# A chunked attention and feed-forward kernel: the second block's first pair is transposed by VectorE, and four small edits at the start

## The chip, the cores and the metric

One Trainium2 chip, one of its cores. The time is that of one execution on the device, in microseconds; the kernel before was timed in three runs. One further execution was profiled, and all rows below come from it. Shorter is better.

## The reference

```python
# q, k, v: 8 batches x 8 heads x 576 tokens x 64, float32
scores = (1 / sqrt(64)) * q_c @ k_c.T          # in chunks of 64 tokens
scores = scores - max(scores, axis=-1)
attn   = exp(scores)
attn   = attn / (sum(attn, axis=-1) + 1e-9)
x      = (attn @ v_c).transpose(...).reshape(4608, 512)
h      = x @ w_in                              # w_in: 512 x 2048, float64
g      = h * (1 / (1 + exp(-1.702 * h)))
out    = g @ w_out                             # w_out: 2048 x 512, float64
```

Attention runs inside chunks of 64 tokens. Its result is the input of a two-layer feed-forward net. The weights come in 8-byte words, and the kernel turns them into a high and a low 4-byte part itself.

## The kernel before, in words

The 4608 tokens are 36 tiles of 128, in 9 blocks of 4 tiles. Every large product is done in three passes (high weight with low data, high with high, low with high). The first three blocks are computed plainly: for each of 16 column tiles j of the hidden layer, `h_j` makes 128 hidden features for 512 tokens (two halves, `h0_j` and `h_j`, six products each, lines L1607 to L1609), ScalarE and VectorE turn them into `g` (steps `gh` and `gl`, L1628, L1629, L1633), and four steps `o_j_t` (L1643 to L1645, three products each) add the second layer's part for tile t. The other six blocks go in pairs of blocks with fewer products; the change does not touch them.

The weights are fetched once, one tile j of `w_in` and one of `w_out` at a time, and are prepared during the first block. A weight's steps are: `raw_j` (SP issues its transfers, L373 and L378), `wsc_j` and `wlow_j` on ScalarE (L382, L389), `wshift_j` and `wj_j` on VectorE (L395, L402), `wh_j` on ScalarE (L418), `w_j` on VectorE (L421). Tiles 0 and 1 are handled in two parts, `raw_0_0` (`w_in`) and `raw_0_1` (`w_out`). `w_15` is the last one, and `h0_15` needs it.

Attention of the first block is done in four units (`plan_first`), of two heads and 512 tokens each: `q_u`, `k_u`, `v_u` are transfers (L507, L528), `tqp_u` and `tkp_u` transposes on TensorE by products with an identity (L541 for units 0 and 2, L549 for units 1 and 3), `s_u` the scores (L579), then the largest value, the subtraction, the exponential, the sum (`s_sum`, which adds `eps` = 1e-9, L596), the normalising on GpSimd, `ep_u` a transpose back (L606), `xp_u` the product with v (L628). Before the first transposes TensorE runs 7 warming products, ident by ident, of 128 columns (`keep_warm`, L1720), whose result nobody uses.

From the second block on, attention goes in pairs u of token tiles, all heads at once (`plan_pair`). The constant `NPE` says which pairs use TensorE for their transposes: those with u below 6, which is pair 4 alone. Pair 4 loads rows of q and k in 4 transfers of 256 KB (L478), transposes them on TensorE in two steps of eight (`tp0_4`, `tp1_4`, L1353), copies the results out (`tq`, L1360 on ScalarE, `tk`, L1363 on VectorE), computes scores (`s_4`, L1387), transposes e with eight products (`ep_4`, L1423) that ScalarE copies out (L1427), and multiplies by v in a step of its own (`xp_4`, L1461). All later pairs load q and k in small pieces of 32 KB (`load_qk`, L1328), so placed that VectorE's 32 x 32 transposes do the rest (`t_dve`, L1371, two instructions; `e_dve`, L1436, eight instructions), and their product with v runs directly behind the scores of the next pair (`s_u` takes `last["x"]` with it) into the two `hp` banks of PSUM.

The order of all steps is one list of names, `ORDER`, written out at the top; each step issues its instructions on its own engine's queue, and every queue runs in order. All transfers are issued by SP. A step only waits for what it reads, and for the buffers that it overwrites; buffers are matched by a tag. The first weight part's buffer for j = 1 has the tag `w1a`.

Of the kernel before, what the change touches and what calls it, by code (L numbers as in the profile page):

```python
# [8 lines left out]
F32 = mybir.dt.float32  # L9
# [5 lines left out]
ALU = mybir.AluOpType  # L15
AX = mybir.AxisListType
# [221 lines left out]
def tile_chunk_attention_ffn(  # L238
# [21 lines left out]
    NB = NTL // TB  # L260
    BT = TB * P
    SCALE = 1.0 / float(D) ** 0.5
    NPE = 6
    NTMP = 3
    WARM = 7
    FILL = ()
# [1519 lines left out]
```

## Time and profile before

| | us |
|---|---|
| median of three runs (lowest, highest) | 813.99 (812.33, 816.24) |
| the profiled execution's own time | 814.22 |
| its span, first to last instruction | 812.4 |
| TensorE busy | 803.3 |
| VectorE busy | 595.0 |
| ScalarE busy | 380.3 |
| GpSimd busy | 90.0 |

The engine's busy time is the time in which it has an instruction running; the ends of matmuls are modelled. The share of TensorE is 99%, of VectorE 73%, of ScalarE 47%, but these are means over stages that differ. The granted clock of TensorE is 1.0 in every slice that the page shows.

### The profile page before, as it was taken

The numbers are of one execution on the slowest core, as the hardware profiler recorded it, in microseconds if no ns is written. First come the engines' busy times: TensorE is split into PE (matmuls) and PEld (weight loads), VectorE is DVE, ScalarE is ACT, GpSimd is POOL, SyncE is SP. The second block draws the span as 40 slices with busy tenths as digits, with TensorE's granted clock in tenths as the row PEclk, the third lists the DMA queues.
The fourth block names the chain that finished last, engine by engine and source line by source line (L and its number), as shares of the span: only waits on it lengthen the run. The fifth ranks groups of instructions, "written<-read, shape, count | busy, mean of one in ns | idle before, by whom it ended". The sixth has DMA issues, their size and how long they took to land.

```text
span 812.4 us, 15467 instructions
## 1 busy us (share of the span) xinstructions
PE 803.3 (99%) x5934; PEld 666.6 (82%) x5934; DVE 595.0 (73%) x900; ACT 380.3 (47%) x610; POOL 90.0 (11%) x83
## 2 busy tenths in 40 slices
PE   7999999999999999999999999999999999999998
PEld 6788888888888888888888888888888888888887
DVE  4888974646567979886787888876878545659965
ACT  5998934334445546413345451523554512338450
POOL 1100004030045651000000010000001000000000
PEclk9999999999999999999999999999999999999999
DMA  9995646642366677667664538676533046766433
GB/s 266 301 349 127 160 94 182 166 97 52 66 186 169 172 198 215 179 184 216 180 159 130 133 80 217 178 215 192 156 118 105 0 128 193 230 202 220 134 100 105
DMA packets 240106, 133.17 MB, mean 164 GB/s; under 512 B 179104, under 2 KB 207776, under 8 KB 240032
## 3 DMA queue, kind: packets, MB, share of 16 engines
q1 hardware_dynamic: 240032, 132.18, 58.0%
q8 instruction: 47, 0.77, 0.4%
q14 instruction: 27, 0.22, 0.1%
HBM read 97.52 MB, written 32.51 MB: 160 GB/s over the span
## 4 chain that ended last, share of the span: by engine, by line
PE 97%; DMA 1%; ACT 0%; issue 0%; DVE 0%; SPq 0%; DVEq 0%
PE po L1643 13%; PE po L1645 13%; PE po L1644 13%; PE hp L867 9%; PE hp L869 9%; PE hp L868 9%; PE hp L1607 5%; PE hp L1609 5%; PE hp L1608 5%; PE acc_A L1133 3%; PE acc_B L1133 3%; PE s L1387 2%; PE x L1461 2%; PE acc_A L1126 2%; PE acc_B L1126 1%; DMA first_a<-in_k_dram 1%
## 5 line engine op out<-in xcount | busy, mean ns | idle before, releaser
L1643 PE MATMUL po<-w,g_l 128*128 128x512 f32 x448 | 176.4, 394 | 0.0
L1645 PE MATMUL po<-w,g_h 128*128 128x512 f32 x448 | 174.5, 390 | 0.0
L1644 PE MATMUL po<-w,g_h 128*128 128x512 f32 x448 | 174.5, 389 | 0.0
L1643 PEld LDWEIGHTS po<-w,g_l 128*128 128x128 f32 x448 | 84.1, 188 | 18.4 <-DVE g_l L918 0.4
L1645 PEld LDWEIGHTS po<-w,g_h 128*128 128x128 f32 x448 | 84.1, 188 | 17.6
L1644 PEld LDWEIGHTS po<-w,g_h 128*128 128x128 f32 x448 | 84.1, 188 | 16.9
L867 PE MATMUL hp<-w,w 128*128 128x512 f32 x224 | 87.5, 390 | 0.1
L869 PE MATMUL hp<-w,w 128*128 128x512 f32 x224 | 87.2, 389 | 0.0
L868 PE MATMUL hp<-w,w 128*128 128x512 f32 x224 | 87.2, 389 | 0.0
L1436 DVE STREAM_TRANSPOSE eT<-e 32x512 f32<-32x512 f32 x120 | 84.2, 702 | 3.1 <-POOL e L1417 1.2
L1417 POOL TENSOR_TENSOR e<-e,r 128x1024 f32<-128x1024 f32 x16 | 31.5, 1968 | 436.4 <-DVE r L1414 338.9
L1607 PE MATMUL hp<-x_l,w 128*128 128x512 f32 x184 | 72.1, 392 | 0.0
L1608 PE MATMUL hp<-x_h,w 128*128 128x512 f32 x184 | 71.6, 389 | 0.0
L1609 PE MATMUL hp<-x_h,w 128*128 128x512 f32 x184 | 71.6, 389 | 0.0
L1628 ACT ACTIVATE hp<-hp 128x512 f32<-128x512 f32 x48 | 28.0, 584 | 81.6 <-PE hp L1609 71.5
L1633 DVE TENSOR_TENSOR g_l<-hp,g_h 128x512 fp32r<-128x512 f32 x48 | 33.0, 688 | 44.9 <-ACT g_h L1629 44.6
L867 PEld LDWEIGHTS hp<-w,w 128*128 128x128 f32 x224 | 42.1, 188 | 9.9 <-issue 0.5
L869 PEld LDWEIGHTS hp<-w,w 128*128 128x128 f32 x224 | 42.0, 188 | 8.7
L868 PEld LDWEIGHTS hp<-w,w 128*128 128x128 f32 x224 | 42.0, 188 | 8.6
L867 PE MATMUL hp<-w,pieces 128*128 128x512 f32 x112 | 43.7, 390 | 0.0
L869 PE MATMUL hp<-w,pieces 128*128 128x512 f32 x112 | 43.6, 389 | 0.0
L868 PE MATMUL hp<-w,pieces 128*128 128x512 f32 x112 | 43.6, 389 | 0.0
(225 smaller groups left out, 1473.3 us busy)
## 6 DMA issues: line engine op xcount, KB each, us to landing
w<-seven SPq DMA_DIRECT2D x112, 256.0 KB, 3.1
pieces<-seven SPq DMA_DIRECT2D x56, 256.0 KB, 3.2
seven<-w SPq DMA_DIRECT2D x24, 512.0 KB, 3.7
raw<-in_moe_w_in_dram SPq DMA_DIRECT2D x16, 512.0 KB, 7.2
raw<-in_moe_w_out_dram SPq DMA_DIRECT2D x16, 512.0 KB, 6.9
four<-four_w SPq DMA_DIRECT2D x32, 256.0 KB, 3.5
raw<-in_q_dram SPq DMA_DIRECT2D x208, 32.0 KB, 2.2
raw<-in_k_dram SPq DMA_DIRECT2D x208, 32.0 KB, 2.2
```

Of the source, the lines that this page charges most:

```text
L867: nc.tensor.matmul(hp, w[:, 0, c], xl[:, c], start=c == 0, stop=False)
L868: nc.tensor.matmul(hp, w[:, 0, c], xh[:, c], start=False, stop=False)
L869: nc.tensor.matmul(hp, w[:, 1, c], xh[:, c], start=False, stop=c == 1)
L1133: nc.tensor.matmul(halves(o), gh[:, c], w, start=first, stop=stop, skip_group_check=not fresh)
L1436: nc.vector.transpose(st["et"][po : po + 32, :, 32 * a : 32 * a + 32], st["e"][pi : pi + 32, :, 32 * b : 32 * b + 32],)
L1607: nc.tensor.matmul(hp, wh, xl, start=cc == 0, stop=False)
L1608: nc.tensor.matmul(hp, wh, xh, start=False, stop=False)
L1609: nc.tensor.matmul(hp, wl, xh, start=False, stop=cc == NCC - 1)
L1633: nc.vector.tensor_tensor(gl, h_t[g], gh.bitcast(F32), op=ALU.subtract)
L1643: nc.tensor.matmul(po, gl[:, c], w[:, 0, :], start=first, stop=False)
L1644: nc.tensor.matmul(po, gh[:, c], w[:, 0, :], start=False, stop=False)
L1645: nc.tensor.matmul(po, gh[:, c], w[:, 1, :], start=False, stop=last)
```

## The change

Seven edits in one:

1. `NPE` goes from 6 to 4. Pair 4 takes the way of the later pairs: 32 small transfers for q and k, transposes on VectorE, its product with v behind the scores of pair 6. The list loses `rows0_4`, `rows1_4`, `tp0_4`, `tp1_4`, `tk0_4`, `tk1_4`, `ep_4`, `xp_4` and gains `qk_0_0_4` to `qk_1_3_4`, `et0_4` to `et2_4`, `hp0_6`, `hp1_6`.
2. The warming becomes 14 products of 64 columns.
3. A tile `hold` with the tag `w1a` gets a copy of the lower right quarter of the identity. The last transposing product of k_0 reads it, so the transfer `raw_1_0`, whose buffer has the same tag, cannot start before that product is done. The step also names `tkp_0` as a need.
4. `eps` becomes a part of a larger tile; the sums of the first block are reduced into row 0 of a two-row view whose row 1 holds 1e-9, and a second reduction adds the rows, in place of an addition.
5. The need of a pair's transposes on those of the pair before is dropped for pair 4, which no longer has one before it on that path.
6. Part 0 of weight 0 becomes the first weight that is loaded.
7. `ORDER` is written anew from end to end. Its transfers begin: before `q_0 k_0 k_1 q_1 raw_1_0 q_2 k_2 k_3 q_3 raw_2 v_0 v_1 raw_0_0 v_2 v_3`, after `q_0 k_0 q_1 k_1 raw_0_0 q_2 k_2 k_3 raw_1_0 q_3 raw_2 v_1 v_0 raw_0_1 qk_0_0_4 v_2 v_3`. TensorE's steps begin: before `warm tqp_0 tkp_0 tkp_1 tqp_1 s_0 s_1 tqp_2 tkp_2 tkp_3 tqp_3 s_2 s_3`, after `warm tqp_0 tkp_0 tqp_1 tkp_1 s_0 tqp_2 s_1 tkp_2 tkp_3 tqp_3 s_2 s_3`. The rest of the list differs in many places by a step or two.

```diff
-    NPE = 6
+    NPE = 4
...
-    WARM = 7
+    WARM = 14
...
-    eps = pad.tile([P, 96], F32, tag="pad", name="eps")[:, :16]
+    small = pad.tile([P, 96], F32, tag="pad", name="small")
+    eps = small[:, :16]
+    zeps = small[:, 32:64].rearrange("p (r c) -> p r c", r=2)
...
-    nc.vector.memset(eps, 1e-9)
+    nc.vector.memset(small, 1e-9)
+    hold = const.tile([P, 1024], F32, tag="w1a", name="hold")[:, :CH]
+    nc.vector.tensor_copy(hold[CH:], ident[CH:, CH:])
...
-            plan.add(DMA, (n, 1.5, 384), at - 5.5, load, need=slot_users(j), make=e("raw"), take=[tag])
+            plan.add(DMA, (n, 1.5, 384), at - 5.5, load, need=slot_users(j) + ["tkp_0"] * (name == "1_0"), make=e("raw"), take=[tag])
...
-                            nc.tensor.matmul(to, data, ident[r, r], start=True, stop=True)
+                            last = (u, i, t, h, half) == (0, 1, TB - 1, 1, 1)
+                            nc.tensor.matmul(to, data, hold[r] if last else ident[r, r], start=True, stop=True)
...
-            nc.vector.tensor_reduce(z, st["e"], axis=AX.X, op=ALU.add)
-            nc.vector.tensor_tensor(z, z, eps[:, :NK], op=ALU.add)
+            nc.vector.tensor_reduce(zeps[:, 0, :NK], st["e"], axis=AX.X, op=ALU.add)
+            nc.vector.tensor_reduce(z, zeps[:, :, :NK].rearrange("p r c -> p c r"), axis=AX.X, op=ALU.add)
...
-        warm = pool.tile([P, P], F32, tag=tag, name="warm")
+        warm = pool.tile([P, CH], F32, tag=tag, name="warm")
         for _ in range(count):
-            nc.tensor.matmul(warm, ident, ident, start=True, stop=True)
+            nc.tensor.matmul(warm, ident, ident[:, :CH], start=True, stop=True)
```

## Rows read from the trace of the kernel before

**Rows 1.** The page: busy time and instructions of each engine; an instruction queue.

```profile
PE 803.3 (99%) x5934; PEld 666.6 (82%) x5934; DVE 595.0 (73%) x900; ACT 380.3 (47%) x610; POOL 90.0 (11%) x83
...
q8 instruction: 47, 0.77, 0.4%
```

**Rows 2.** Windows, first 26 us: length, then busy us of PE, PEld, DVE, ACT, POOL.

```profile
0.00:26.00 26.00, 20.25 (x478) 17.24 (x482) 14.43 (x32) 15.69 (x26) 4.87 (x10) 1.00 0.90 265
```

**Rows 3.** Waits of PE over the whole span: total, times, longest.

```profile
PE qkTp L541 <- issue: 2.0, 1, 2.0
```

**Rows 4.** Chain that ended last, 8 to 20 us: start, us, what.

```profile
11.67 1.98 issue
```

**Rows 5.** Timeline of PE and SP, first 20 us: start, us, instructions, idle before.

```profile
1.36 3.36 PE L1720 MATMUL warm<-ident 128*128 128x128 f32 x14 [1.36 <-POOL ident masks.py:199]
...
5.21 0.67 SPq L507 DMA_DIRECT2D first_a<-in_q_dram  x1
6.99 1.97 PE L549 MATMUL qkTp<-ident,first_a 128*64 128x128 f32 x32 [1.00 <-DMA first_a<-in_k_dram]
...
8.06 4.79 SPq L528 DMA_DIRECT2D first_b<-in_v_dram  x4
...
19.62 0.69 PE L628 MATMUL x<-first_b 64*64 64x64 f32 x32 [0.25 <-ACT first_b L613]
```

**Rows 6.** Windows: busy PE, PEld, DVE, ACT, POOL; clock, DMA share, GB/s.

```profile
30.00:116.00 86.00, 85.99 (x684) 70.80 (x683) 73.39 (x87) 70.68 (x88) 4.14 (x3) 1.00 0.70 205
50.00:60.00 10.00, 10.00 (x104) 8.11 (x104) 9.64 (x11) 9.33 (x12) 0.00 (x0) 1.00 1.02 363
80.00:100.00 20.00, 20.00 (x148) 16.40 (x147) 18.63 (x21) 18.80 (x22) 0.00 (x0) 1.00 0.67 180
64.00:68.00 4.00, 4.00 (x19) 3.30 (x19) 3.09 (x6) 3.96 (x6) 1.91 (x1) 1.00 0.33 53
26.00:30.00 4.00, 4.00 (x36) 3.20 (x26) 4.00 (x7) 3.89 (x8) 0.00 (x0) 1.00 1.00 342
```

**Rows 7.** Chain that ended last, at the detours of pairs 4 and 8.

```profile
31.06 0.88 PE qkTp L1353 x8
...
31.95 0.50 PE hp L1607
...
68.30 0.23 PE po L1645
68.53 0.87 PE eTp L1423 x8
...
75.54 1.09 PE x L1461 x64
76.63 0.43 PE hp L1607
...
113.27 0.93 PE x L1461 x64
```

**Rows 8.** Timeline of DVE and PE around the last weight tile.

```profile
114.60 1.23 DVE L421 TENSOR_TENSOR w<-wtmp,w 128x1024 fp32r<-128x1024 f32 x1 [1.12 <-ACT w L418]
...
116.09 0.39 PE L1645 MATMUL po<-w,g_h 128*128 128x512 f32 x1
116.48 0.50 PE L1607 MATMUL hp<-x_l,w 128*128 128x512 f32 x1
```

**Rows 9.** Groups of instructions of VectorE, first 116 us: busy, mean ns, idle before.

```profile
L1436 DVE STREAM_TRANSPOSE eT<-e 32x512 f32<-32x512 f32 x8 | 5.6, 697 | 0.1
L1371 DVE STREAM_TRANSPOSE qkT<-raw 128x1024 f32<-128x1024 f32 x4 | 4.8, 1230 | 0.0
L1363 DVE COPY qkT<-qkTp 128x512 f32<-128x512 f32 x2 | 1.4, 683 | 0.0
```

**Rows 10.** Line L1328: issue of a small transfer, ns min/median/max.

```profile
L1328 SPq DMA_DIRECT2D raw<-in_k_dram x208: 312/449/2570, 62.0 to 559.0; - x104
```

**Rows 11.** The page: transfers, KB each, median us from issue to landing.

```profile
first_b<-in_v_dram SPq DMA_DIRECT2D x8, 128.0 KB, 5.0
```

More of the change, by code (lines that the diff above doesn't have):

```diff
@@ L1517, in plan_pair @@
                 plan.add(
-                    DVE, 1.14, rank, lambda i=i: t_dve(i), need=raw[i * NP : i * NP + NP] + ([ev("tq0")] if i else [f"tq1_{u - 2}"]),
+                    DVE, 1.14, rank, lambda i=i: t_dve(i), need=raw[i * NP : i * NP + NP] + ([ev("tq0")] if i else [f"tq1_{u - 2}"] * (u > TB)),
                     make=ev(f"tq{i}"), take=[] if i else ["tr"], give=[raw_tag] if i else (),
```

350 rows, old and new, of the table ORDER are left out of this document.

## The prediction

> **What bounds the kernel now.** I read the page first: TensorE is busy for 803.3 of 812.4 us [rows 1], so little can be won but less TensorE work, or less idle time at the two ends. The windows put 5.75 of the 9.1 us of idleness into the first 26 us (26.00 minus 20.25) [rows 2]; the other 3.4 lie nearly all behind the last product, in the last addition and store, where the change only shuffles a few steps, and I leave them as they are. At the start the waits and the chain name the largest piece: 2.0 us of "issue" inside the transposes of unit 2 (L541), from 11.67 on [rows 3, 4]. "Issue" is a wait for nothing that the profile shows. By the code TensorE had then run 14 warming records and 64 + 32 + 64 + 48 more, 222, each with its own weight load, so 444 instructions; the page has 47 transfers of 16 KB on an instruction queue, and 2 x 5934 instructions over 47 transfers is one per 252 [rows 1]. I therefore take the 1.98 us for a late code transfer that shared the DMA engines with weights. A further 1.0 us is the wait for the k of unit 1, until 6.99 [rows 5].
>
> From 26 us on TensorE has no gap, but VectorE has little room: in the stretch 30 to 116 us, in which all weights are split and the second block's attention runs, it is busy 73.4 of 86 us while TensorE is busy 85.99 [rows 6]. The last weight tile shows how close this is: VectorE finishes w_15 at 114.60 + 1.23 = 115.83, and h_15 starts at 116.48, 0.39 after the start of a product that normally hands over after 0.23 [rows 7, 8]: it waits 0.16 us. So before 116 us a saving on TensorE is worth only what VectorE can follow.
>
> **The change part by part.** The sum is made against the profiled execution, 814.22 us (span 812.4 and 1.8 around it), 0.23 above the median of 813.99.
>
> Pair 4 leaves TensorE's transposes. A detour is worth its chain pieces plus what the next product takes beyond the usual 0.23 [rows 7]: the first eight transposes 0.88 + (0.50 - 0.23) = 1.15; the second eight have no such follower and are like the eight of e, 0.87 each. The products x_4 stood alone, 1.09 + (0.43 - 0.23) = 1.29; they now ride behind s_6, where the same 64 cost 0.93, so 0.36 less. Together 3.25 us of TensorE work, all of it before h_15.
>
> What it adds on VectorE: eight 32-row transposes of e at 0.697 (5.6) and two of q and k at 1.230 (2.5), less two copies of 0.683 (1.4): 6.7 us more, all of it in the order ahead of w_15 [rows 9]. ScalarE loses three copies. x_4 now leaves through both hp banks; the pairs after it do so in the chain with no wait, so nothing is put down for it [rows 7].
>
> VectorE decides what the 3.25 us are worth. It has 86 - 73.4 = 12.6 us idle in the stretch. For the full gain it must do 73.4 + 6.7 = 80.1 us of work in 86 - 3.25 = 82.75, which is 97% busy. Its densest rows are 9.64 of 10 us (96.4%) and 18.63 of 20 (93.2%) [rows 6]. At 96.4% the work takes 83.1 us, a gain of 2.9; at 93.2% it takes 85.9, a gain of 0.1. I take the middle, 95%: 84.3 us, a gain of 1.7, with 0.1 and 3.25 as ends.
>
> The loads of pair 4's q and k become 32 transfers of 32 KB in place of 4 of 256 KB. SP issues such a one in 0.449 us [rows 10], 14.4 us in all, spread between weight loads; the DMA engines need more too: the stretch with only such transfers moved 53 GB/s at a share of 0.33, so 161 GB/s at full share against 342 [rows 6], that is 6.5 us in place of 3.1 for 1.05 MB. These 3.4 us fall where the DMA share is 1.0 and delay weights; no ScalarE or VectorE step of the weights waits for its transfer now (they wait for one another, as w_15 does), so I price them at nothing and keep up to 3.4 us for the case that this cover goes.
>
> The first 26 us. The warming becomes 14 products of half the width. Seven of 128 columns took 3.36 us [rows 5]; with time by columns 14 of 64 take the same, with time by product twice that. The bounds are 3.4 and 6.7 us, and I take 3.4, since records of the same shape later need only 0.87 / 8 = 0.11 each [rows 7] where these took 0.24, so it is the streaming and not the number of them that was slow. Up to 1.0 us more would vanish in the wait that ends at 6.99. The Trainium skill (TensorE: Matmul & The Clock Gate, section "The mechanism") says a weight load overlaps running products only where the row groups differ; with full-array weights each product then costs load plus stream, and by its figures (section "LDWEIGHTS") the warming would take an estimated 4.5 us, still inside that wait. The 0.24 us of the warming row fits that rule and the hidden load alike, and the sum is 811.5 us by both.
>
> The 28 more instructions ahead of the first transposes move the code boundary of instruction 444 to the start of tkp_2, and TensorE asks for that code a little sooner. The held-back load adds a wait on SP: raw_1_0 starts only when the last transposed product of k_0 is done, near 6.0 us, where SP issued q_3 at 5.21 [rows 5]; q_3, raw_2 and the v of units 1 and 0 stand behind it. For that time no weight is put in front of the code transfer. The stall can go by 0 to 2.0 us. But a half-megabyte weight now also stands ahead of q_3 and v: 1.5 to 2 us. The four v issues ended at 8.06 + 4.79 = 12.85 [rows 5] and such a transfer lands 5.0 us after its issue [rows 11], at 17.9; that becomes about 19.5, and x of unit 0 ran at 19.62 [rows 5]. So what the stall gives is mostly taken back by v. I take 1.0 us, between 0 and 2.0.
>
> The Trainium skill (DMA: Bandwidth & Descriptors, section "Queues, rings and completion order") says each DMA engine takes turns between its queue rows, a packet at a time. By that rule the code transfer does not stand behind SP's backlog and holding a weight back buys nothing; the sum would lose its 1.0 us. The 1.98 us row fits queueing better, but shows no queue.
>
> The 1e-9 as a second row: a small addition becomes a reduction of 16 values, four times; the larger memset and the copy into "hold" run before VectorE has its first input, the transposes of unit 1, which start at 6.99 [rows 5]. Nothing either way.
>
> Sum: 814.2 - 1.7 - 1.0 = 811.5 us.
>
> **The rivals.** *All of it arrives.* VectorE reaches 97% and the code stall goes whole: 814.2 - 3.25 - 2.0 = 808.9. For it: TensorE went through 50 to 60 us without a gap while VectorE was at 96.4% [rows 6]. Against it: no row shows VectorE at 97% for 80 us.
>
> *VectorE takes the gain back.* It stays at 93% and the v transfers or the code transfer eat the start: 814.2 - 0.1 - 0 = 814.1. The row of 80 to 100 us speaks for it.
>
> *Slower: VectorE's idle time doesn't shrink.* Its queue is in order, and its 12.6 us are waits for ScalarE and TensorE results; if they stay, w_15 comes 6.7 us later, h_15 starts at 123.2, the removed TensorE work only becomes waiting, and the time is 814.2 + 6.7 = 820.9. It decides from the point where more than 5.9 us of the 12.6 remain idle (12.6 - 6.7: above this h_15 starts later than now); each further us costs one. For it: h_15 waits for w_15 even now. Against: ScalarE has less to do, and much of the idleness is VectorE waiting for a TensorE that is behind it.
>
> *The warming takes twice as long.* 3.36 us more, of which the wait of 1.0 before 6.99 takes up 1.0: 811.5 + 2.4 = 813.9.
>
> **How the numbers follow.** Forecast 0.42 (809.9 to 813.2); all arrives 0.28 (807.8 to 809.9); taken back 0.15 (813.2 to 815); slower 0.09 (815 to 821); doubled warming 0.06. A measurement here can tell about 0.5% (4.1 us, so 809.9 and 818.1) from no change. Faster by more: the second case and a sliver of the first, 0.33. Slower by more: the far half of the slower case, 0.05. Within: 0.62. The range leaves out the lower edge of "all arrives" and most of "slower": 807.8 to 815.8.
>
> **What would show it.** TensorE's total should fall by about 3.2 us, with 24 transposes of 128 columns gone; if not, the first step is wrong. The "issue" wait in L541 or its neighbours should be under 1.5 us. VectorE from 30 us to the end of w_15 should be about 95% busy; h_15 should start near 113.5 to 114. TensorE waits on w (L421) or g_l before 116 us, over 4 us in sum, would mean the slower case. A wait of x (L628) for v would confirm the price of the hold. Matmul starts 0.24 us apart in the warming mean that it doubled.

## The result, and the profile after

The changed kernel takes 819.76 us (median of six runs, 818.58 to 821.50); the kernel before, on the same chip, 814.73. The ratio is 1.0077, with an interval of 1.0062 to 1.0092: slower, by 5 to 7.5 us. (The ratio is not that of the two medians, which is 1.0062; here and below the two can lie 0.15% apart.) The forecast was 811.5, and the range ended at 815.8. The profiled execution took 820.12 us, with a span of 818.3 against 812.4.

The page after, in the lines that answer to [rows 1], and the windows that answer to [rows 2, 6] (length; busy us of PE, PEld, DVE, ACT, POOL; clock, DMA share, GB/s):

```profile
PE 807.6 (99%) x5924; PEld 669.5 (82%) x5924; DVE 601.3 (73%) x909; ACT 378.8 (46%) x607; POOL 93.2 (11%) x83
```
```profile
0.00:26.00 26.00, 21.86 (x426) 20.18 (x426) 12.75 (x30) 14.53 (x24) 4.69 (x10) 0.99 0.83 240
30.00:116.00 86.00, 85.19 (x643) 68.58 (x646) 78.53 (x96) 68.48 (x84) 4.60 (x2) 1.00 0.75 209
```

TensorE has lost 24 transposes, and yet it is busy 4.3 us longer. VectorE is busy 78.5 us between 30 and 116 us in place of 73.4, and TensorE, which had no gap there, now has 0.8 us of them. The waits of TensorE over the span (total, times, longest):

```profile
PE po L1650 <- DVE g_l L1640: 2.3, 3, 1.7
PE eTp L613 <- POOL first_b L608: 2.0, 2, 1.8
...
PE hp L1614 <- DVE x_l L1482: 0.4, 1, 0.4
```

The gaps over 0.15 us between 30 and 120 us are waits for VectorE: for a g_l at 74 and at 105 us (0.24 and 0.39), and for the x_l of h_15 at 119. The longest ones lie elsewhere, 1.8 us at 23 us (for GpSimd) and 1.7 at 295 us. The issue wait of [rows 3] is gone. The start is told by the timeline of TensorE (start, us, instructions, idle before), to be read against [rows 5]:

```profile
1.36 6.24 PE L1727 MATMUL warm<-ident 128*128 128x64 f32 x28 [1.36 <-POOL ident masks.py:199]
...
9.45 3.22 PE L556 MATMUL qkTp<-ident,first_a 128*64 128x128 f32 x32
...
25.14 0.66 PE L613 MATMUL eTp<-ident,first_b 128*128 128x128 f32 x4 [1.82 <-POOL first_b L608]
...
27.40 1.92 PE L635 MATMUL x<-first_b 64*64 64x64 f32 x64
```

The warming has the 28 records of 0.22 us, nearly as long as those of twice the width before (0.24). The transposes of unit 1 (L556) take 3.22 us where they took 1.97 [rows 5], and the same line later in this kernel takes 1.97 again. Behind the wait of 1.82 us, 64 products of L635 take 1.92 us (1.45 before). The windows there show why: the granted clock is at half, the lower of the two levels (1.2 GHz), from 25.7 to 29.1 us.

```profile
25.00:26.00 1.00, 0.86 (x6) 0.77 (x6) 1.00 (x3) 1.00 (x4) 0.98 (x2) 0.85 0.58 227
26.00:27.00 1.00, 1.00 (x5) 0.76 (x4) 1.00 (x3) 1.00 (x3) 0.14 (x1) 0.50 1.05 312
27.00:28.00 1.00, 1.00 (x25) 0.67 (x26) 1.00 (x3) 0.60 (x2) 0.00 (x0) 0.50 0.72 144
28.00:29.00 1.00, 1.00 (x49) 1.00 (x48) 0.84 (x1) 1.00 (x3) 0.00 (x0) 0.50 0.93 271
29.00:30.00 1.00, 1.00 (x19) 0.85 (x12) 0.77 (x2) 0.84 (x4) 0.00 (x0) 0.94 1.00 354
```

The last weight tile, which [rows 8] had ending at 115.83, ends at 117.35 + 1.22 = 118.57, and h_15 starts at 119.23 where it started at 116.48 [rows 8], 2.75 us later. The timelines of VectorE, with the wait for ScalarE's part as before, and of TensorE there:

```profile
117.35 1.22 DVE L427 TENSOR_TENSOR w<-wtmp,w 128x1024 fp32r<-128x1024 f32 x1 [1.13 <-ACT w L424]
```
```profile
119.23 0.50 PE L1614 MATMUL hp<-x_l,w 128*128 128x512 f32 x1 [0.39 <-DVE x_l L1482]
```

Counting equal products of the two layers in both traces, it stays 2.7 to 2.8 us behind to 190 us and is 3.2 us behind at 273 us, and at 295 us it loses another 2 us in one place. The timeline of VectorE (the lines left out are small):

```profile
284.07 1.21 DVE L1418 TENSOR_REDUCE z<-e 128x16 f32<-128x1024 f32 x1
...
286.24 2.13 DVE L723 TENSOR_TENSOR w<-xs,w 128x512 fp32r<-128x512 f32 x1
288.30 1.78 DVE L773 TENSOR_TENSOR w<-sums,w 128x512 fp32r<-128x512 f32 x1
290.00 5.71 DVE L1443 STREAM_TRANSPOSE eT<-e 32x512 f32<-32x512 f32 x8
295.74 0.69 DVE L1640 TENSOR_TENSOR g_l<-hp,g_h 128x512 fp32r<-128x512 f32 x1
```
and of TensorE:
```profile
294.44 0.39 PE L1652 MATMUL po<-w,g_h 128*128 128x512 f32 x1
296.49 0.50 PE L1650 MATMUL po<-w,g_l 128*128 128x512 f32 x1 [1.66 <-DVE g_l L1640]
```

A g_l for which TensorE stands idle from 294.8 on stands in VectorE's queue behind all eight transposes of pair 18. From there on the distance stays between 5.1 and 5.8 us, and the span is 5.9 us longer.

### The profile page after: what moved, and what is told of

Its sections match the earlier page's. It is cut to its first block, busy times and chain, and to the rows that moved or that the text cites. A ratio compares the mean times of both kernels' runs of the same rounds, so it can differ in the third digit from the quotient of the medians.

```text
span 818.3 us, 15481 instructions
## 1 busy us (share of the span) xinstructions
PE 807.6 (99%) x5924; PEld 669.5 (82%) x5924; DVE 601.3 (73%) x909; ACT 378.8 (46%) x607; POOL 93.2 (11%) x83
## 4 chain that ended last, share of the span: by engine, by line
PE 88%; DVE 4%; ACT 3%; SPq 2%; DMA 2%; issue 1%; POOL 1%; DVEq 0%; POOLq 0%; ACTq 0%
PE po L1650 11%; PE po L1651 11%; PE po L1652 11%; PE hp L874 9%; PE hp L875 9%; PE hp L876 9%; PE hp L1614 4%; PE hp L1616 4%; PE hp L1615 4%; PE acc_A L1140 3%; PE acc_B L1140 3%; PE s L1394 2%; PE acc_A L1133 2%; PE x L1468 2%; SPq L1335 1%; PE acc_B L1133 1%
## 5 line engine op out<-in xcount | busy, mean ns | idle before, releaser
L1443 DVE STREAM_TRANSPOSE eT<-e 32x512 f32<-32x512 f32 x128 | 89.8, 702 | 9.4 <-POOL e L1424 7.2
```

Of the source, the lines that this page charges most:

```text
L1443: nc.vector.transpose(st["et"][po : po + 32, :, 32 * a : 32 * a + 32], st["e"][pi : pi + 32, :, 32 * b : 32 * b + 32],)
```

## The experiments

All times are medians, with the ratio to the kernel before, run beside it on the same chip, and its interval. The changed kernel has 1.0077 on this scale; 0.1% is 0.8 us. An interval is some 1 us wide to either side, so a difference between two versions of less than 1 to 2 us is not shown by the times alone; where it is told, a trace has to carry it.

### The start: warming and hold

```diff
-    WARM = 14
+    WARM = 7
-        warm = pool.tile([P, CH], F32, tag=tag, name="warm")
+        warm = pool.tile([P, P], F32, tag=tag, name="warm")
-            nc.tensor.matmul(warm, ident, ident[:, :CH], start=True, stop=True)
+            nc.tensor.matmul(warm, ident, ident, start=True, stop=True)
```


> The changed kernel with its warming put back to 7 products of 128 columns. Theory A (the warming's cost goes by products and everything behind it starts later by as much): the warming row falls from 6.24 us back to about 3.4, unit 1's transposes start near 7.2 when their k lands (9.45 now), and the time falls by 2.3 to 2.9 us, to about 817. Rival (from 30 us on VectorE decides, and it catches up): the time stays within 1 us of the changed kernel, about 819.5, with longer waits for g_l. Second rival: the 28 records fewer bring the code stall of 2 us back, and the gain is under 1 us.

816.80 us, 1.0042 (1.0028 to 1.0055): 2.9 us less than the changed kernel, as theory A has it. The warming row is 3.35 us, and the clock between 26 and 30 us is 1.00 though a wait of 1.3 us for the same GpSimd step is still there.

```diff
-    hold = const.tile([P, 1024], F32, tag="w1a", name="hold")[:, :CH]
-    nc.vector.tensor_copy(hold[CH:], ident[CH:, CH:])
...
-need=slot_users(j) + ["tkp_0"] * (name == "1_0")
+need=slot_users(j)
...
-nc.tensor.matmul(to, data, hold[r] if last else ident[r, r], start=True, stop=True)
+nc.tensor.matmul(to, data, ident[r, r], start=True, stop=True)
```


> The changed kernel without the held-back weight: no hold tile, no wait of raw_1_0 for the transposes. Theory A (the hold delays transfers by 2 to 4 us, but no TensorE instruction of the first 26 us waits for one of them): SP goes on at 5.2 in place of 9.6, the time stays within 1 us of the changed kernel, 819 to 820.5. Rival B (the hold starves the weights and v, and so leads to the idle time at 25 us and the lower clock behind it): the wait of 1.8 us and the stretch at 0.5 clock go, 3 us faster, about 816.5. Rival C (the hold kept the code transfer free): an issue stall of about 2 us is back, about 821.5.

819.33 us, 1.0073 (1.0057 to 1.0089): no difference from the changed kernel. The half clock is still there (0.77 between 26 and 30 us), so the hold did not lead to it; the issue wait is 0.2 us, so the hold took no more than that here.

> The changed kernel with both undone: 7 warming products of 128 columns and no held-back weight, so the start's edits are gone and pair 4, the order and the 1e-9 as a row are left. If the two add up: 817 by theory A alone, 814 if the hold costs 3 us too. If the forecast's price of pair 4 (1.7 us gained) was right and the start was all that went wrong, the time is near 813, below the kernel before. If VectorE's added 6.7 us are what it costs, it stays above 817.

(Both edits above.) 816.91 us, 1.0035 (1.0022 to 1.0049): as with the warming alone. Now an issue wait of 1.5 us is back; it was 0.8 in e1. With the long warming TensorE comes later to this place, and the wait is nearly gone with or without the hold; with the old warming the two traces don't tell what the hold does (e15 and e13 below have the same first 122 us as e3 and e1, and waits of 0.2 and 0 us). And the kernel is still slower than before: the start's edits aren't all of it.

The same two edits, each put alone into the kernel before (the first by the diff of e1 the other way round):

> The kernel before with one edit of the change: 14 warming products of 64 columns. Theory A (each product costs the same at 64 and at 128 columns, and the start has no room for it beyond the wait of 1.0 us for k): the warming takes 6.24 us, unit 1's transposes start near 9.4 in place of 6.99, and the time rises by 2 to 3.5 us, to 816 to 817. Rival: the later TensorE meets code and data that are already there, the issue stall of 2.0 us goes, and the time stays within 1 us of the kernel before.

816.89 us, 1.0052 (1.0035 to 1.0069): slower by 2.8 to 5.6 us, as theory A has it. The timeline of its TensorE shows both halves, the doubled warming and the stall that shrinks from 2.0 to 0.5 us:

```profile
1.36 6.23 PE L1720 MATMUL warm<-ident 128*128 128x64 f32 x28 [1.36 <-POOL ident masks.py:199]
...
14.89 0.69 PE L541 MATMUL qkTp<-ident,first_a 64*64 64x64 f32 x30 [0.49 <-issue]
```

```diff
+    hold = const.tile([P, 1024], F32, tag="w1a", name="hold")[:, :CH]
+    nc.vector.tensor_copy(hold[CH:], ident[CH:, CH:])
...
+need=slot_users(j) + ["tkp_0"] * (name == "1_0")
+nc.tensor.matmul(to, data, hold[r] if last else ident[r, r], start=True, stop=True)
```


> The kernel before with one edit of the change: raw_1_0 held back behind the last transposing product of k_0. Here q_2, k_2, k_3 and q_3 stand behind it on SP, so they are issued 3 us later. Theory A (as the comparison with and without it in the changed kernel has it): nothing comes of it either way, within 1 us of the kernel before. Rival: with no weight on the DMA engines when the code is asked for, the issue stall of 2.0 us goes and the kernel gets 1.5 to 2 us faster, about 812.

814.91 us, 1.0020 (1.0009 to 1.0030): slower by 0.7 to 2.4 us, where theory A expected nothing and the rival a gain. The stall goes as the rival says, and two waits for the q and k of unit 2 stand in its place, since these are behind raw_1_0 on SP, which stood still from 2.7 to 6.06 us:

```profile
10.57 0.69 PE L544 MATMUL qkTp<-ident,first_a 64*64 64x64 f32 x32 [0.70 <-DMA first_a<-in_q_dram]
12.01 0.69 PE L544 MATMUL qkTp<-ident,first_a 64*64 64x64 f32 x32 [0.74 <-DMA first_a<-in_k_dram]
```

```diff
-k_1 q_1 tkp_0 raw_1_0 tkp_1 tq_0 q_2 tk_0 tqp_1 k_2 xa_1 k_3
+k_1 q_1 tkp_0 tkp_1 tq_0 q_2 tk_0 tqp_1 k_2 xa_1 k_3 raw_1_0
```


> The kernel before with raw_1_0 moved behind k_3 in the order and held back behind the last transposing product of k_0, so that q_2, k_2 and k_3 no longer stand behind it on SP. Theory A (the hold took the issue stall away, but the q and k of unit 2 then came late): with both out of the way the stall of 2.0 us goes and no wait for q or k takes its place, and the kernel is 1 to 2 us faster than before, 811.5 to 812.5. Rival (weights or v, now later, are waited for instead): within 1 us of the kernel before.

815.03 us, 1.0019 (1.0008 to 1.0030): slower by as much, so neither expectation came. No stall; but now the scores of unit 2 wait 1.5 us, and those of unit 3 0.7, for copies made by ScalarE. Its timeline shows the work on the late weight ahead of the copy for unit 2, whose transposes TensorE had ended at 11.3 us:

```profile
11.95 0.66 ACT L381 ACTIVATE raw<-raw 128x512 f32<-128x512 f32 x1 [2.94 <-DMA raw<-in_moe_w_in_dram]
...
14.24 1.00 ACT L561 ACTIVATE first_a<-qkTp 128x1024 f32<-128x1024 f32 x1
```

In both versions other waits take the place of the stall's 2 us. What the stall is, the traces' transfers on the instruction queue (q8 in [rows 1]) show: in the first 14 us there is one such transfer, of 16 KB, and in all eleven traces that have an issue wait in the transposes this wait ends 1.3 to 1.6 us after it has landed (in the kernel before it landed at 12.16 and TensorE went on at 13.65). The hold brings it forward: it starts at 6.7 us in e6 and 7.6 in e12, against 10.0 to 11.2 in five traces with the old start, the old warming and no hold.

### VectorE and pair 4

The changed kernel with the warming of e1, and in `e_dve`:

```diff
+                if u == 4:
+                    nc.gpsimd.memset(st["et"], 0.0)
+            if u == 4:
+                return
```


> The changed kernel with 7 warming products of 128 columns, and of pair 4 the eight transposes of e on VectorE left out (GpSimd clears the tile instead, so the output of two token tiles is wrong). VectorE has 5.6 us less to do before the last weight tile, nearly as before the change, while TensorE keeps its saving. Theory A (VectorE's added work takes back what TensorE saves, in the waits for g_l and x_l at 69, 94, 100 and 114 us): most of these waits go and the time falls by 1.5 to 2.5 us against the same kernel with the transposes, to about 814.5; the wait at 290 us stays. Rival (the waits come from the new order, not from the amount of work): they stay, and the time is 816.8.

815.87 us, 1.0019 (1.0009 to 1.0028), against 1.0042 (1.0028 to 1.0055) with them: the 5.6 us of VectorE work cost 1.9 us by these ratios, whose intervals just meet. In its trace the gaps of TensorE at 69, 94 and 100 us are gone, 0.7 us in all between 60 and 118 us; those at 114 (behind w_15) and 290 us stay, and this execution has one of 1.2 us at 37 us. Windows of e1 and then of this kernel (length, busy us of PE, clock, DMA share, GB/s):

```profile
60.00:118.00 58.00, 56.90 (x480) 1.00 0.64 162
```
```profile
60.00:118.00 58.00, 57.63 (x491) 1.00 0.69 177
```

```diff
-    NPE = 6
+    NPE = 4
     ORDER: rows0_4 -> qk_0_0_4 ... qk_0_3_4; rows1_4 -> qk_1_0_4 ... qk_1_3_4;
            tp0_4 tk0_4 tp1_4 tk1_4 ep_4 xp_4 out; et0_4 et1_4 et2_4 et_4, hp0_6 hp1_6 in; s_6 behind gl_11
```


> The kernel before with the first edit of the change alone: pair 4 goes the way of the later pairs, set into the old order by hand (small loads where the two row loads of q and of k stood, et0_4 behind gl_7, et1_4 behind w_8, et2_4 behind gl_8, et_4 behind gl_9, the products with v behind s_6, which moves behind gl_11). Old start, old warming, no hold, old order elsewhere. Theory A (pair 4's own trade: TensorE 2.8 us less, of which VectorE's transposes take 1.9 back): 0.5 to 1.5 us faster than before, 812.3 to 813.5. Rival (the new order was needed for it: w_15 or a g_l comes late behind the 6.7 us): 1 to 4 us slower, with waits for g_l, x_l or w before 120 us. Second rival: all of it arrives, 811.

826.06 us, 1.0139 (1.0117 to 1.0160): far slower than either theory had it. By 59 us it already stood 7.8 us behind the kernel before, ahead of the first transpose of e; a stretch at half clock from 50.6 to 57.4 us, which begins in the wait of 2.8 us shown below, is in that. SP's timeline, and the first of the waits between 26 and 60 us:

```profile
19.42 11.71 SPq L1326 DMA_DIRECT2D raw<-in_q_dram  x16
...
33.24 10.58 SPq L1326 DMA_DIRECT2D raw<-in_k_dram  x16
```
```profile
ACT raw L380 <- DMA raw<-in_moe_w_out_dram: 7.7, 2, 5.3
...
PE hp L1605 <- ACT w L416: 2.8, 1, 2.8
```
Sixteen small transfers in a row hold SP for 11 us, and the weights behind them are waited for: the cover under which the prediction priced them at nothing is their place between the weight parts.

```diff
     ORDER, beside the above:
+qk_0_0_4 raw_1_1 qk_0_2_4 ... raw_3 qk_0_3_4 raw_4 qk_0_1_4 ... raw_5 qk_1_3_4 ... raw_8 qk_1_1_4
+raw_7 qk_1_0_4 ... gh_2 tq0_4 ... raw_9 qk_1_2_4 ... w_5 tq1_4 raw_11 qk_0_0_6
```


> As the kernel before with pair 4 alone on VectorE, but its 32 small transfers stand four at a time between the weight parts, as in the changed kernel, and not in two blocks of sixteen; tq0_4 and tq1_4 follow later (behind gh_2 and w_5). Theory A (in the version with the blocks, SP needed 11.7 and 10.6 us to issue sixteen of them, and the weights behind came late: 7.8 of its 12 us were lost by 58 us, ahead of the first transpose of e): most of these 12 us go, 813 to 817, with waits for g_l, x_l or w before 120 us of 3 us at most in sum. Rival (the old order of VectorE can't take the 6.7 us): still over 820 us.

824.93 us, 1.0152 (1.0132 to 1.0171): no better. ScalarE no longer waits for the weights' transfers, but the scores of pair 4, still at their old place, wait for its last loads and their transposes:

```profile
PE s L1384 <- DVE qkT L1368: 4.3, 1, 4.3
```

The clock is at half here too, from 54.7 to 61.6 us, and at 79 and 84 us TensorE waits 2.3 us for VectorE's step on a weight, as it did in e16.

So "pair 4 alone" has no price of its own: it needs loads, transposes and scores to move together, as the changed kernel's order does. An order made for it with the old start wasn't found.

### The order behind 120 us

```diff
-et1_18 h0_45 gh_44 psum_6 et2_18 ld2_0_0 h_45 v1_18 po_5 qk_1_1_22 et_18 o_43_1 o_43_3 gl_44
+et1_18 h0_45 gh_44 psum_6 gl_44 et2_18 ld2_0_0 h_45 v1_18 po_5 qk_1_1_22 et_18 o_43_1 o_43_3
```


> The changed kernel with one name of the order moved: gl_44 stands before et2_18 and not behind et_18, so that VectorE makes this g_l after four of the eight transposes of pair 18. Theory A (the one wait of 1.66 us at 294.8, with the 0.3 behind it, is lost for good, since TensorE has no gap to catch up in behind it): 1.5 to 2.0 us faster than the changed kernel, about 818, and no wait over 0.5 us behind 200 us. Rival: the wait comes back at the next g_l or at the pair's products, and the time stays at 819.8.

818.48 us, 1.0056 (1.0040 to 1.0071): 1.7 us less, which the intervals alone don't separate from the changed kernel, but with the g_l between two groups of four transposes and no wait there:

```profile
289.64 2.84 DVE L1439 STREAM_TRANSPOSE eT<-e 32x512 f32<-32x512 f32 x4
292.51 0.69 DVE L1636 TENSOR_TENSOR g_l<-hp,g_h 128x512 fp32r<-128x512 f32 x1
293.24 2.86 DVE L1439 STREAM_TRANSPOSE eT<-e 32x512 f32<-32x512 f32 x4
```

Why that g_l is late at all was asked from both sides:

```diff
-gh_42 z_18 pa_7 h_43 n_18 v0_18 ... gl_42 ... gh_43 h_44 gl_43
+gh_42 pa_7 h_43 v0_18 ... gl_42 ... gh_43 z_18 h_44 gl_43 n_18
```


> The kernel before with two names of the order moved: z_18 behind gh_43 and n_18 behind gl_43, where the changed kernel has them (one block of products later). Theory A (the wait of 1.7 us at 294 us in the changed kernel is made by the order alone, not by pair 4 or the start): TensorE waits 1 to 2 us for the g_l of block 44 behind the transposes of pair 18, and the time rises by 1 to 2 us. Rival: without the delay of the changed kernel there is no wait and the time does not move.

814.15 us, 1.0010 (1.0001 to 1.0018): the rival. The wait at 290 us is there, but it has 0.2 us.

```diff
-gh_42 t3x_0_0 o_41_0 phi0_5 gl_42 ... gh_43 z_18 ... gl_43 n_18
+gh_42 z_18 n_18 t3x_0_0 o_41_0 phi0_5 gl_42 ... gh_43 ... gl_43
```


> The changed kernel with z_18 put back behind gh_42 and n_18 directly behind it (one block of products earlier, as in the kernel before); warming and hold as changed. Theory A (the wait at 294 us comes of z_18's late place together with the two VectorE instructions that run slowly beside GpSimd behind it): the wait falls under 0.5 us and the time falls by 1.3 to 2 us, to about 818. Rival (only the two slow instructions set it): about 1 us of the wait stays, and the time falls by 0.5 us or less.

819.09 us, 1.0063 (1.0050 to 1.0076): some 1.1 us less, within the noise, with 0.6 us left of the wait, so in between. The late z_18 is a part of the wait, and by the rows above the two additions of 2.13 and 1.78 us, which take 0.68 us elsewhere, are the rest (argued, not tried).

The whole second half of the order was then exchanged at gl_16 (about 122 us), in both directions:

```diff
     ORDER (with WARM = 7 and 128 columns):
-new list
+new list up to gl_16, then the remaining steps as the old list has them
```


> The changed kernel with 7 warming products of 128 columns, whose order is the new one up to gl_16 (about 122 us) and from there on that of the kernel before (the same steps). Theory A (pair 4's saving does arrive, some 1.4 us by 138 us, and is lost again behind 200 us to the new order, in the waits of 0.3 us at 200, 2.05 us at 290 and 0.6 to 1.3 us at 362): 2.5 to 3.5 us less than with the warming alone put back, 813 to 814, at or just below the kernel before. Rival (the tail of the old order waits in the same places, since the front now hands over with VectorE late): 816 to 817.

814.96 us, 1.0016 (1.0004 to 1.0028), against 1.0042 with the new second half: 2.1 us less, and still above the kernel before, where theory A had it level or below.

```diff
     ORDER of the kernel before:
-old list
+old list up to gl_16, then the remaining steps as the new list has them
```


> The kernel before, with the new order only from gl_16 on (about 120 us), all else as before: no pair 4 on VectorE, old warming, no hold. Theory A (the new order behind 120 us costs by itself): waits of about 2 us near 290 and of 0.5 to 1.3 us near 362 us, 2 to 3.5 us slower than before, 816 to 817.5. Rival (it costs only with the change's other parts): within 1 us of the kernel before.

815.68 us, 1.0026 (1.0014 to 1.0038), against 1.0000 with the old one. The new second half costs 0.26%, 2.1 us, on either front, and its trace has the same wait, though neither pair 4 nor the start was touched:

```profile
292.50 0.50 PE L1640 MATMUL po<-w,g_l 128*128 128x512 f32 x1 [1.75 <-DVE g_l L1630]
```

(The edit of e13, and the hold out as in e2.)

> As the version with the new order up to gl_16 and the old one behind, with the held-back weight taken out too: what is left of the change is pair 4 on VectorE, the new order of the first 122 us, the first part of weight 0 first and the 1e-9 as a row. Theory A (the hold gains nothing, and costs up to 1.4 us where q or k stand behind it): 812.5 to 814, level with or up to 1 us below the version with the hold and the kernel before. Rival (the hold keeps the code transfer free): an issue stall of 1.5 to 2 us makes it 814.5 or more.

815.74 us, 1.0024 (1.0009 to 1.0039): within the interval of the version with the hold. The issue wait is 0.2 us here too. The two theories are not told apart; 814.5 or more came out, but not by the stall that the rival gave for it. Ten of its twelve runs have a mean granted clock of 0.998 or less, and the profiled one is at half clock from 22.1 to 25.5 us.

### Two tries at something better

```diff
     ORDER (with WARM = 7 and 128 columns):
+gh_7 gl_7 et0_4 ... xh_4 xl_4 mx_6 ... gh_12 ex_6 w_13 gl_12 z_6 ... psum_6 gl_44 et2_18
+wshift_15 wj_15 et2_6 ... gh_14 wh_15
```


> The changed kernel with 7 warming products of 128 columns and five places of the order changed so that no g_l, x_l or last weight stands behind VectorE work that is not needed yet: gl_44 before et2_18; gh_7 and gl_7 before et0_4; xh_4 and xl_4 before mx_6; gh_12 before ex_6 and gl_12 before z_6; wj_15 behind wshift_15 and wh_15 behind gh_14. Pair 4 stays on VectorE. Theory A (the waits behind 60 us are made by the places in VectorE's queue): the waits at 70, 94, 100, 114 and 290 us go, 3 to 4.4 us less than with the warming alone put back, 812.5 to 814. Rival (VectorE has too much work before w_15): they come back elsewhere before 116 us, only the one at 290 us is won, and the time is near 815.

818.49 us, 1.0067 (1.0054 to 1.0079): worse than e1 (1.0042). The waits at 94, 100 and 290 us are gone, and a new one for a g_l at 107 us costs 2.9 us, behind which the clock fell to half for some 3 us.

(The same without the last line.)

> The changed kernel with 7 warming products of 128 columns and four places of the order changed: gl_44 before et2_18; gh_7 and gl_7 before et0_4; xh_4 and xl_4 before mx_6; gh_12 before ex_6 and gl_12 before z_6. This is the earlier version with the fifth place (wj_15, wh_15) left as it is, since that one brought a wait of 2.9 us for a g_l at 107 us. Theory A: the waits at 94, 100 and 290 us go as they did there, and the one at 114 us stays: 2.5 to 3 us less than with the warming alone put back, 813.8 to 814.5, level with the kernel before. Rival (VectorE has too much work before the last weight): what is won before 116 us comes back there, and the time is near 815.

818.56 us, 1.0061 (1.0039 to 1.0084). The profiled execution was the slowest, 823.44. The wait of 2.9 us is still there, so the fifth place was not its cause; which one is wasn't tried. No version ran faster than the kernel before.

## Why the prediction was wrong

The miss is 9.0 us: a gain of 2.7 was forecast, and the ratio gives a loss of 6.3.

**The warming** was the step that failed first: "I take 3.4, since records of the same shape later need only 0.87 / 8 = 0.11 each [rows 7] where these took 0.24, so it is the streaming and not the number of them that was slow". It was the number. A record of 64 columns takes 0.22 us and one of 128 columns 0.24 [rows 5], and in both kernels they start 0.213 us apart; the row that I used against it came from later in the run, when everything goes at twice the pace. The later fast records say nothing of what sets the slow pace. The change measured 6.24, beyond the 4.5 that I had estimated from the Trainium skill (TensorE: Matmul & The Clock Gate, section "LDWEIGHTS") too; and those 4.5 were 1.1 more than 3.4, a little more than the wait of 1.0 that I let them vanish in.

The long warming also keeps TensorE slow behind it. The first clock record of the trace, which grants the full clock, begins at 12.05 us in the changed kernel and at 5.09 in the kernel before; in the five traces with 14 products of 64 columns it begins between 10.3 and 12.1 us, in the fourteen with 7 of 128 between 4.2 and 7.0. Cost of all this: 2.9 us (e1); alone in the kernel before, 2.8 to 5.6 (e5). The rival "takes twice as long" had the doubled row and, at 2.4 us, nearly the size; I gave it 0.06. The late rise of the clock stood in no case.

No case had the half clock at 26 us either. In five of six runs the changed kernel shows a mean clock of 0.998 or less, with the old warming (e1) one of five, and the kernel before in seven of 104; these seven have a median of 815.7 us, the other 97 one of 813.7. But the old warming doesn't keep it away: e6 has five of twelve such runs and e15 ten of twelve. In the traces it stands behind several waits of TensorE near 20 us; which of them decide isn't settled, since e1 and e3 have the wait for GpSimd too and stay at full clock.

**The code stall** went whole, where half was put down, and the traces bear out that it was a late code transfer, as I took it to be (the stall ends 1.3 to 1.6 us after a transfer on the instruction queue has landed). In the changed kernel the hold gave little of it: without the hold and with the long warming the stall is 0.2 us (e2), since TensorE comes to this place some 3 us later. In the kernel before the hold does remove it, and q and k come late by 1.4 us instead (e6). That "what the stall gives is mostly taken back" was right; by v it was not: no product waited for v in the changed kernel.

**Pair 4** on TensorE was sized at 3.25 us. TensorE is busy for 803.2 to 804.8 us in three traces with the old first part (before, e7, e14) and for 800.9 to 803.2 in four with the new one and the old warming (e1, e3, e13, e15): 1.7 us less by their means. VectorE's side went to the low end of its bounds (0.1 to 3.25), and this is the second step that failed: in e13 TensorE is idle from 60 to 118 us for 58 − 56.64 = 1.4 us, where it had no gap (a window of e13: length, busy us, clock, DMA share, GB/s),

```profile
60.00:118.00 58.00, 56.64 (x480) 1.00 0.64 162
```

and the eight transposes of e cost 1.9 us (e9). The sign that I had named decides it: h_15 was to start near 113.5 to 114. It starts at 115.2, 115.4 and 116.5 us in the three traces with the old first part, and at 115.1, 115.3, 116.1 and 116.2 in the four with the new one and the old warming, 115.7 by the mean of either. So of the 1.7 us nothing is left at h_15 that stands out of the spread between executions. The densities that I took as a limit, 93 to 96%, were not reached: in the changed kernel VectorE was 91% busy (78.53 of 86) and TensorE waited all the same, 0.2 to 0.4 us at a time, each time for one g_l or x_l that came late in VectorE's queue. VectorE itself was waiting ahead of them: at 70 us 1.79 us for GpSimd, with the g_l behind the transposes that needed it,

```profile
72.07 1.42 DVE L1443 STREAM_TRANSPOSE eT<-e 32x512 f32<-32x512 f32 x2 [1.79 <-POOL e L1424]
73.52 0.69 DVE L1640 TENSOR_TENSOR g_l<-hp,g_h 128x512 fp32r<-128x512 f32 x1
```

at 103 us 0.81 for ScalarE's g_h, and at 116 us 1.13 for ScalarE's part of w_15. That is the mechanism of the rival "VectorE's idle time doesn't shrink", at a small size. A mean share over 80 us doesn't show it.

**The small transfers** were priced at nothing with 3.4 us "for the case that this cover goes". In the changed kernel the cover held: the waits name no product that waited for a weight before 116 us. e16 shows what it hides when it goes, 7.8 us by 59 us.

**The order** is the step that failed without having a term. "The rest of the list differs in many places by a step or two" stood in the description, and the sum had nothing for it beyond 116 us. It costs 2.1 us there (e13, e14), nearly all in one wait at 290 us; from the start of h_15 to the end of the span the old order takes 695.7 to 696.7 us in four traces (before, e5, e13, e15), the new one 698.0 to 700.7 in five (changed kernel, e1, e2, e3, e14). TensorE has no gap for hundreds of us, so nothing can catch up.

**The 1e-9 as a row** costs nothing that shows: the second reduction takes 0.17 us (L603), as the addition in its place did (L596 of the kernel before).

Together: 2.9 for the warming, 2.1 for the order behind 120 us, and 4.0 between the forecast gain of 2.7 and the 1.3 us that e13 still loses. The 2.7 did not arrive: with the old warming h_15 starts no sooner than before, pair 4's part being lost to VectorE's waits and the stall's part to other waits at the start. The 1.3 us are in part the half clock: e13's profiled execution, at full clock, has the span of the kernel before, 812.4; four of its twelve runs have a mean clock of 0.998 or less and a median of 815.9 us, the other eight 814.4, and the kernel before beside them, in its runs above 0.998, 813.6. What makes the last 0.8 us isn't settled.

## What to carry to other kernels

When a row could be read as "per column" or "per instruction", ask for a second row of the same stretch with another width, and keep both readings near even if there is none; a row from a faster stretch doesn't decide it. Where an engine has no gap for hundreds of us, every instruction that it needs must stand in its maker's queue ahead of long work that can wait; a list of steps that is written anew from end to end has a cost of its own, to be looked for even where the work is the same. And a busy share of 91% on the engine behind does not mean that there is room.

## What the runs showed of the hardware that I had not expected

- **The first products run at the pace of the lower clock, and the windows don't show it.** The trace's clock records begin with the rise to the full clock, at 5.09 us in the kernel before and at 12.05 in the changed one; the windows count the time ahead of the first record as 1.00, and so do the page's slices. The pace tells: the warming's records start 0.213 us apart, at 64 columns as at 128, and four transposes of 128 columns (L613 at 26.42) start as far apart in the windows at 0.50, but 0.109 apart at full clock. The transposes of unit 1 change from 0.213 to 0.110 us for a pair of records at 12.06 us in the changed kernel, and in e2 and e5 at 10.79 and 10.33, where the first clock record begins too (10.79 and 10.31). So they took 3.22 us in the changed kernel, 2.60 in e2, 2.37 in e5 and 1.97 in the kernel before, with no wait inside.
- **The half clock behind short waits.** In the changed kernel TensorE worked 1.55 and 1.80 of two us each from 18 to 22, then 1.01 of two, then none of one, and the clock was 0.50 in the three windows from 26 to 29 us. In e6, e9 and e15, with the old warming, it was at half from about 22 to 25 us. The kernel before had a wait of 1.98 us at 11.7 [rows 4], and no row shows its clock lower behind it.
- **VectorE beside GpSimd.** The addition L723 takes 2.13 us and L773 1.78 where both have a median of 0.68; GpSimd's timeline in the changed kernel has these beside them (that they are the cause wasn't tried):

```profile
285.93 1.91 POOL L1424 TENSOR_TENSOR e<-e,r 128x1024 f32<-128x1024 f32 x1 [0.61 <-DVE r L1421]
287.79 3.45 POOL L753 TENSOR_TENSOR whole<-w 128x512 f32<-128x512 f32 x2
```

The transposes behind, of 0.71 us each, run beside GpSimd too (four of its additions, of 0.74 us each, from 291.3) and are hardly longer than in [rows 9] (0.697).
